# Attention with a mixture of experts on one core: one-hots and low parts move from GpSimd to VectorE, the heads' sums to GpSimd, half of the early weight bounds to ScalarE

## The chip, the cores and the metric

The kernel runs on one NeuronCore of one Trainium2 chip. The core has a matrix engine (TensorE; the profile calls it PE, and its weight loads PEld), VectorE (DVE), ScalarE (ACT), GpSimd (POOL) and SyncE (SP), which issues most DMAs. The metric is the device time of one execution in microseconds (us), as the median of several runs.

## The reference

A windowed attention is followed by a mixture of experts in which each token goes to two of eight experts.

```python
# attention: q, k, v are (8 batches, 8 heads, 576 positions, 64)
scores = scale * q @ k.T                       # per head
mask = (rel >= 0) & (rel < 128)                # rel = query position - key position
scores = where(mask, scores - slope_h * |rel|, -1e9)
attn = softmax(scores);  out = attn @ v
x = out as 4608 tokens of 512                  # heads side by side
# experts
logits = x @ w_gate
noisy = logits + log1p(exp(x @ w_noise)) * noise
top2 = the two largest of 8;  weights = softmax of the two
for e in range(8):                             # w1[e]: 512 x 1024, w2[e]: 1024 x 512
    h = relu(x[tokens of e] @ w1[e])
    out[tokens of e] += weight * (h @ w2[e])
```

## The kernel before, in words

**The order of the work.** The instructions of all engines are laid out by a planner inside the kernel's own code (class `Order`). Every piece of work is a generator, a "strand", that yields operations, each with an engine, a cost in us that the author wrote beside it, and a rank. The planner keeps a clock of its own, and whenever an engine is free by that clock it emits the waiting operation with the lowest rank. The order in which it emits becomes the fixed order of each engine's queue on the chip. An engine works its queue in order, so an operation whose input is late holds up all that stands behind it. The costs and the constants at the top of the file (`GATE`, `ROUTE`, `WEIGHTS`, `STAGE`, `LATE` and so on, which shift ranks) thus set the order, but not how long anything takes. The helper `either` offers an operation to ScalarE and VectorE; the first that is free takes it, and an entry of `LATE` shifts VectorE's rank for it. `move` is a DMA on SP.

**Attention.** There are 32 pairs (a batch and two heads) of three groups of query blocks, 96 units (`unit`). Each unit makes its scores on TensorE (L472, L479), takes tops with the mask and bias on VectorE (L495 to L505), exponentials with their sums on ScalarE (L512), transposes on TensorE (L519), an evacuation on either engine (L261 or L265, into `pT`), a split of the diagonal blocks on GpSimd (`split`, L539 and L540), and the weighted sum of values on TensorE (L560). When all four head pairs of a group are there, `rows` adds a small number to the sums of exponentials on GpSimd (L632) and takes reciprocals on VectorE (L635). Then `row_major` writes the tokens to HBM (L660 to L668), and `gate` makes the logits of each head on TensorE (L683), evacuates and transposes them (L694), multiplies by the reciprocals on VectorE (L699, into `lt`), and adds the eight heads up in one VectorE reduction (L704, into `lg`).

**Routing.** For each of the eight batches, `route` takes the noise and the logits, finds the two best experts and each token's place in the expert's list. The places are written as one-hots, in two parts: which line of the list (80 values, `hot[0]`, L783 and L788) and which place in the line (64 values, `hot[1]`, L793), the latter multiplied by the token's number. For batches 0 to 6 GpSimd makes them in ten operations each, one for each of five token blocks and two choices; for the last batch VectorE makes the lines in one operation and the places in ten. Ten matmuls (`list_`, L798) multiply the two one-hots into lists, which VectorE takes out (`whole_numbers`, L803 to L806) and an indirect DMA adds to the lists in HBM (L877). The planner counts 2.2 us for the lines on GpSimd and 0.4 us for each of five pairs of places.

**Experts.** Weights and tokens are split into a high and a low 16-bit part, and each product is three matmuls (high by high, high by low, low by high). To scale weights into range, the largest absolute value of each expert's `w1` and `w2` is taken first: for experts 0 and 1 by `early_sizes`, 16 pieces of 128x512 each, and for the rest by `size_of_weights`. Each piece is loaded (L1013) and reduced on VectorE (`largest`, L1014); `powers_of_weights` turns the maxima into powers of two (L1029 and on). Then `scaled_weight` loads each chunk f = 0 to 7 of the expert (L1039), makes its high part on ScalarE or VectorE (L261 or L263), and its low part: for expert 0 on GpSimd in two operations (L1045, L1046), for the others on VectorE in one (L1051).

Once six batches are routed, a first wave takes two blocks of 384 tokens of expert 0 and works on them beside the end of attention; the second wave takes all other tokens of all experts. For a block, tokens are gathered by indirect DMA (L1062), scaled (`fit`, L1075 to L1079) and transposed (L1093); L1107 is the first product, L1127, L1129 and L1142 its ReLU in two parts, L1151 or L1156 the second product, and L1228 the indirect DMA that adds the result to the output.

**Ranks that the change and the prediction's steps touch.** A unit's rank is about its place in 160 (five per pair) plus an entry of `STAGE`. Routing of batch b has rank 20b - `ROUTE`. Chunk f of expert 0 has rank `WEIGHTS[0]` + `WEIGHTS[1]` f. The first wave starts at rank `FFN0`, the second at 1000.

Of the kernel before, what the change touches and what calls it, by code (L numbers as in the profile page):

```python
# [21 lines left out]
NQ = 5  # L22
# [18 lines left out]
GATE = (-9.0, -7.0)  # L41
ROUTE = -11.5
SCATTER = (15.0, -1042.6, -45.1)
FFN0, FFN1 = 175.6, 182.4
WEIGHTS = (94.1, 13.2)
TOKENS = 75.6
STAGE = (-14.6, 12.0, 2.3, -11.7, 15.1, 9.4, 15.1, -33.6)
MIDDLE = 41.4
RESULT = -72.8
SIZES = (65.9, 147.7, 901.7)  # L50
EARLY = 2
SOON = 2.3
TIGHT = (1, 5, 7)
LATE = (-8.0, -9.8, 75.9, 24.8, 4.9, -85.3, 60.4, -97.2, 42.9, 0.5, 26.7, -30.3)
LAG = 0.2
SWITCH, NEAR = 0.093, 3.6
# [165 lines left out]
def attention_moe(ctx: ExitStack, tc: tile.TileContext, qk_, v, w_gate, w_noise, noise, w1, w2,  # L222
# [449 lines left out]
    def gate(b, blocks, xu, den, t, done):  # L672
# [19 lines left out]
        def turn():  # L692
# [11 lines left out]
        yield dve(0.36 if nz == 1 else 0.5, rank, lambda: nc.vector.tensor_reduce(  # L704
            lgs[b % 2][0:rows, i:i + nz], lt[0:rows, 0:nz].rearrange("p z h e -> p z e h"), axis=AX.X, op=OP.add))
# [16 lines left out]
    def route(b):  # L722
# [6 lines left out]
        on, G = (dve, nc.vector) if b == B - 1 else (pool, nc.gpsimd)  # L729
# [49 lines left out]
        def which_line():  # L779

            if b == B - 1:
                shape = [128, 2 * NQ, E * SPAN]
                V.tensor_tensor(hot[0], ef.rearrange("p i k -> p (i k)")[:, :, None].to_broadcast(shape),  # L783
                                steps_[:, None, :].to_broadcast(shape), op=OP.is_equal)
                return
            for i in range(NQ):
                for k in range(2):
                    G.tensor_scalar(hot[0][:, 2 * i + k], steps_, ef[:, i, k:k + 1], None, op0=OP.is_equal)  # L788

        def which_place(i):  # L790

            for k in range(2):
                G.tensor_scalar(hot[1][:, 2 * i + k], steps_[:, 0:LINE], d[:, i, k:k + 1], numbers[:, i:i + 1],  # L793
                                op0=OP.is_equal, op1=OP.mult)
# [72 lines left out]
        yield on(0.98 if b == B - 1 else 2.2, rank, which_line)  # L867
        for i in range(NQ):
            yield on(0.4, rank, lambda: which_place(i))
# [16 lines left out]
        if b + 1 == CUT:  # L886
# [11 lines left out]
            for blk in first:  # L898
                blk.ix, blk.at = (v[:, blk.s0 // 128:(blk.s0 + blk.n) // 128] for v in (ix, cl))
                mark(blk.ids)  # L900
                spawn(weights_back(blk, rank))

# [80 lines left out]
    def early_sizes():  # L983

        yield biased[NP - 1]
        for e in range(EARLY):
            done = Event(16)
            for f in range(8):
                for z, (rg, src) in enumerate(((raw1, w1), (raw2, w2))):
                    t = yield (rg, SIZES[e])  # L990
                    v = t.rearrange("p a b -> p (a b)") if z == 0 else t
                    spawn(largest(rg, t, v, 0.6, SIZES[e], wam[:, e % 2, z, f:f + 1],
# [491 lines left out]
```

## Time and profile before

| | us |
|---|---|
| median of 3 runs | 1205.41 (1204.83 to 1205.69) |
| profiled execution, its own time | 1203.02 |
| its span, first to last instruction | 1201.1 |
| TensorE busy | 1111.9, 93% |
| VectorE busy | 696.6, 58% |
| ScalarE busy | 493.9, 41% |
| GpSimd busy | 432.4, 36% |
| mean granted TensorE clock | 0.968 of full |

The profile is one execution, so sums over its rows are held against its own time of 1203.02 us, not against the median. In rows of groups the columns are line, engine, operation, output and inputs by the program's names with shapes, count; then busy us and mean ns of one; then the idle time of the engine just before these instructions and who ended it. Rows of waits read: who waited for whom, us in total, times, longest. Rows of the timeline begin with start and length in us. In the views by instruction a row gives least, median and greatest duration in ns and the first and last start. A matmul's duration overlaps the next one's.

### The profile page before, as it was taken

The numbers are of one execution on the slowest core, as the hardware profiler recorded it, in microseconds if no ns is written. First come the engines' busy times: TensorE is split into PE (matmuls) and PEld (weight loads), VectorE is DVE, ScalarE is ACT, GpSimd is POOL, SyncE is SP. The second block draws the span as 40 slices with busy tenths as digits, with TensorE's granted clock in tenths as the row PEclk, the third lists the DMA queues.
The fourth block names the chain that finished last, engine by engine and source line by source line (L and its number), as shares of the span: only waits on it lengthen the run. The fifth ranks groups of instructions, "written<-read, shape, count | busy, mean of one in ns | idle before, by whom it ended". The sixth has DMA issues, their size and how long they took to land.

```text
span 1201.1 us, 20775 instructions
## 1 busy us (share of the span) xinstructions
PE 1111.9 (93%) x7192; PEld 649.4 (54%) x7192; DVE 696.6 (58%) x2491; ACT 493.9 (41%) x1327; POOL 432.4 (36%) x676
## 2 busy tenths in 40 slices
PE   7988789876799999999999999999999999999995
PEld 5765556554445444574566456545645654575552
DVE  7989688876666357257535734672584457252310
ACT  7775566644243235133532423342343324232311
POOL 3458978876350230222322032221313220222211
PEclk9999898889799999999999999999999999999998
DMA  8887786412256356335824553472456342332221
GB/s 310 284 285 275 241 306 229 131 45 77 59 122 193 62 141 193 63 75 142 233 40 125 159 126 63 132 218 40 103 173 171 63 132 89 63 62 45 35 27 23
DMA packets 115418, 160.76 MB, mean 134 GB/s; under 512 B 24688, under 2 KB 67952, under 8 KB 115312
## 3 DMA queue, kind: packets, MB, share of 16 engines
q1 hardware_dynamic: 97392, 119.09, 30.4%
q0 software_dynamic: 17920, 40.33, 17.8%
q8 instruction: 57, 0.93, 0.3%
q14 instruction: 49, 0.40, 0.1%
HBM read 117.99 MB, written 41.40 MB: 133 GB/s over the span
## 4 chain that ended last, share of the span: by engine, by line
PE 60%; DMA 5%; DVE 5%; issue 1%; ACT 0%; POOL 0%; another core or an unknown queue 0%; POOLq 0%; DVEq 0%; ACTq 0%
PE bank L1107 28%; PE bank L1151 21%; PE bank L1156 8%; DMA mraw<-in_w_dram 4%; PE bank L1093 2%; DVE wam L1014 2%; DMA raw<-in_w_dram 1%; DVE xl L1100 0%; DMA xg<-xs_dram,ix 0%; PE bank L1209 0%; DVE hl L1142 0%; DMA xg<-xs_dram,cl 0%; DVE yo L263 0%; DVE fit L1079 0%; POOL out_dram L1228 0%
## 5 line engine op out<-in xcount | busy, mean ns | idle before, releaser
L1228 POOL DMA_INDIRECT out_dram<-yo,ix x74 | 116.7, 1577 | 591.5 <-ACT yo L261 438.1
L1142 DVE SCALAR_TENSOR_TENSOR hl<-bank,hh 128x384 f16<-128x384 f32 (+3 forms) x192 | 110.8, 578 | 296.1 <-ACT hh L1127 295.7
L1127 ACT ACTIVATE hh<-bank 128x512 f16<-128x512 f32 (+3 forms) x171 | 87.5, 512 | 364.5 <-PE bank L1107 363.2
L1151 PEld LDWEIGHTS <-hh 128*128 128x128 f16 (+1 forms) x928 | 89.4, 98 | 96.6 <-issue 5.8
L1107 PE MATMUL bank<-xh,w1hb 128*128 128x320 f16 (+2 forms) x384 | 129.9, 338 | 0.0
L1107 PE MATMUL bank<-xl,w1hb 128*128 128x320 f16 (+2 forms) x384 | 129.9, 338 | 0.0
L1107 PE MATMUL bank<-xh,w1lb 128*128 128x320 f16 (+2 forms) x384 | 129.8, 338 | 0.0
L1107 PE MATMUL bank<-xl,w1ha 128*128 128x384 f16 (+3 forms) x384 | 129.7, 338 | 0.0
L1107 PE MATMUL bank<-xh,w1ha 128*128 128x384 f16 (+3 forms) x384 | 129.7, 338 | 0.0
L1107 PE MATMUL bank<-xh,w1la 128*128 128x384 f16 (+3 forms) x384 | 129.7, 338 | 0.0
L512 ACT ACTIVATE p<-p,nm 128x128 f32<-128x128 f32 x288 | 111.6, 391 | 13.2 <-DVE nm L505 13.2
L1107 PEld LDWEIGHTS <-w1ha 128*128 128x128 f16 x768 | 75.3, 99 | 57.4 <-issue 2.8
L1107 PEld LDWEIGHTS <-w1hb 128*128 128x128 f16 x768 | 75.3, 99 | 55.9 <-issue 3.4
L1151 PE MATMUL bank<-w2ha,hl 128*128 128x512 f16 (+1 forms) x234 | 89.3, 382 | 1.2 <-DVE hl L1142 1.2
L1151 PE MATMUL bank<-w2ha,hh 128*128 128x512 f16 (+1 forms) x234 | 89.4, 382 | 0.0
L1151 PE MATMUL bank<-w2la,hh 128*128 128x512 f16 (+1 forms) x234 | 89.3, 382 | 0.0
L1151 PE MATMUL bank<-w2hb,hh 128*128 128x512 f16 x230 | 87.3, 379 | 0.5 <-ACT hh L1127 0.5
L1151 PE MATMUL bank<-w2hb,hl 128*128 128x512 f16 x230 | 87.2, 379 | 0.5 <-DVE hl L1142 0.5
L1151 PE MATMUL bank<-w2lb,hh 128*128 128x512 f16 x230 | 87.2, 379 | 0.0
L560 PE MATMUL bank<-pT,vraw 128*64 128x128 f32 (+2 forms) x896 | 76.4, 306 | 9.6 <-POOL pT L540 9.6
L1062 POOL DMA_INDIRECT xg<-xs_dram,ix x74 | 72.4, 979 | 34.1 <-issue 15.2
L479 PE MATMUL bank<-qk 64*128 64x256 f32 (+1 forms) x512 | 72.4, 404 | 12.8 <-DMA qk<-in_qk_dram 6.5
(220 smaller groups left out, 2173.6 us busy)
## 6 DMA issues: line engine op xcount, KB each, us to landing
raw<-in_w_dram SPq DMA_DIRECT2D x160, 256.0 KB, 4.0
mraw<-in_w_dram SPq DMA_DIRECT2D x48, 512.0 KB, 6.2
qk<-in_qk_dram SPq DMA_DIRECT2D x32, 608.0 KB, 4.9
vraw<-in_v_dram SPq DMA_DIRECT2D x16, 640.0 KB, 6.1
out_dram<-xg SPq DMA_DIRECT2D x10, 1024.0 KB, 7.7
xs_dram<-x SPq DMA_DIRECT2D x32, 256.0 KB, 4.0
xg<-xs_dram,ix POOLq DMA_INDIRECT x74, 4.4
out_dram<-yo,ix POOLq DMA_INDIRECT x74, 5.1
```

The lines of the kernel that those rows point to most:

```text
L479: nc.tensor.matmul(s[h][:, o:o + c], qk[half, i * 128:i * 128 + 128], qk[half, QW + k0:QW + k0 + c], start=True, stop=True)
L512: nc.scalar.activation(pv, pv, AF.Exp, bias=nm[:, z, h:h + 1], scale=-1.0, accum_out=den[:, z, 2 * g + h:2 * g + h + 1])
L560: nc.tensor.matmul(o[half, o0:o0 + c], t[:, kb, hh:hh + D], w, start=m == 0, stop=m == len(lst) - 1)
L1014: yield dve(us, rank, lambda: nc.vector.tensor_reduce(o, v, axis=AX.X, op=OP.max, apply_absolute_value=True))
L1062: yield pool(1.04, rank, lambda: nc.gpsimd.indirect_dma_start(out=xg[0:r], out_offset=None, in_=xs[0:blk.rows], in_offset=bass.IndirectOff ...
L1093: nc.tensor.transpose(a[:, c * 128:c * 128 + r], xg[0:r, c * 128:c * 128 + 128], ident[0:r, 0:r])
L1107: nc.tensor.matmul(t[:, 0:blk.n], wp[:, c], x[:, c, 0:blk.n], start=c == 0 and z == 0, stop=c == 3 and z == 2)
L1127: nc.scalar.activation(o, i, AF.Relu)
L1142: yield dve(0.07 + c * 0.00104, rank - MIDDLE, lambda: nc.vector.scalar_tensor_tensor(hl[:, 0:c], t[:, 0:c], 0.0, hh[:, 0:c], op0=OP.max, ...
L1151: nc.tensor.matmul(blk.y[j][0:r], h[:, cs], wp, start=f == 0 and m == 0, stop=f == 7 and m == 2)
L1156: nc.tensor.matmul(blk.y[c][:, 0:blk.n], wp[:, c * 128:c * 128 + 128], h[:, 0:blk.n], start=f == 0 and m == 0, stop=f == 7 and m == 2)
L1228: ins = nc.gpsimd.indirect_dma_start(out=out, out_offset=bass.IndirectOffsetOnAxis(ap=blk.ix[0:r, j:j + 1], axis=0), in_=t[0:r], in_offset ...
```

## The change

It has five parts, and new values for the constants.

- One-hots: for all batches, VectorE makes the lines in one operation over 10 x 80 values and the places in one over 10 x 64. The numbers are multiplied in by one GpSimd operation (by VectorE in the last batch), in a strand of its own (`number_them`) so that VectorE's lines don't wait for it; the list matmuls wait for both.
- Heads: the eight heads' logits are added up on GpSimd in three additions (8 to 4 to 2 to 1) in place of VectorE's reduction.
- Early bounds: for `w2` of experts 0 and 1, ScalarE takes the sum of absolute values of each row piece in place of VectorE's maximum. A sum is an upper bound of the maximum; the powers of two for these are shifted by 12 to make up for it.
- Low parts of expert 0: made on VectorE in one operation, as for the other experts.
- Costs given to the planner for these, and the constants.

```diff
-GATE = (-9.0, -7.0)
-ROUTE = -11.5
-SCATTER = (15.0, -1042.6, -45.1)
-FFN0, FFN1 = 175.6, 182.4
-WEIGHTS = (94.1, 13.2)
-TOKENS = 75.6
-STAGE = (-14.6, 12.0, 2.3, -11.7, 15.1, 9.4, 15.1, -33.6)
-MIDDLE = 41.4
+GATE = (-9.0, -1.1)
+ROUTE = 3.6
+SCATTER = (15.0, -1042.6, -37.6)
+FFN0, FFN1 = 175.6, 176.6
+WEIGHTS = (97.0, 72.2)
+TOKENS = 68.4
+STAGE = (-4.9, 8.1, 2.3, -7.2, 3.2, 9.4, 8.5, -33.6)
+MIDDLE = 30.8
...
-SIZES = (65.9, 147.7, 901.7)
+SIZES = (77.9, 147.7, 901.7)
-SOON = 2.3
+SOON = 52.3
-LATE = (-8.0, -9.8, 75.9, 24.8, 4.9, -85.3, 60.4, -97.2, 42.9, 0.5, 26.7, -30.3)
+LATE = (-8.0, -35.3, 75.9, 49.7, 15.7, -92.0, 67.3, -97.2, 22.6, 0.5, 26.7, -30.3)
-SWITCH, NEAR = 0.093, 3.6
+SWITCH, NEAR = 0.093, 4.1
...
-        yield dve(0.36 if nz == 1 else 0.5, rank, lambda: nc.vector.tensor_reduce(
-            lgs[b % 2][0:rows, i:i + nz], lt[0:rows, 0:nz].rearrange("p z h e -> p z e h"), axis=AX.X, op=OP.add))
+        def sum_of_heads():
+            for c in (4, 2):
+                v = lt[0:rows, 0:nz, 0:c]
+                nc.gpsimd.tensor_tensor(v, v, lt[0:rows, 0:nz, c:2 * c], op=OP.add)
+            nc.gpsimd.tensor_tensor(lgs[b % 2][0:rows, i:i + nz], lt[0:rows, 0:nz, 0], lt[0:rows, 0:nz, 1], op=OP.add)
+        yield pool(0.7 if nz == 1 else 0.9, rank, sum_of_heads)
...
-        on, G = (dve, nc.vector) if b == B - 1 else (pool, nc.gpsimd)
+        on, G, us = (dve, V, 0.75) if b == B - 1 else (pool, nc.gpsimd, 1.5)
...
         def which_line():
-            if b == B - 1:
-                shape = [128, 2 * NQ, E * SPAN]
-                V.tensor_tensor(hot[0], ...)
-                return
-            for i in range(NQ):
-                for k in range(2):
-                    G.tensor_scalar(hot[0][:, 2 * i + k], steps_, ef[:, i, k:k + 1], None, op0=OP.is_equal)
-        def which_place(i):
-            for k in range(2):
-                G.tensor_scalar(hot[1][:, 2 * i + k], steps_[:, 0:LINE], d[:, i, k:k + 1], numbers[:, i:i + 1],
-                                op0=OP.is_equal, op1=OP.mult)
+            shape = [128, 2 * NQ, E * SPAN]
+            V.tensor_tensor(hot[0], ef.rearrange("p i k -> p (i k)")[:, :, None].to_broadcast(shape),
+                            steps_[:, None, :].to_broadcast(shape), op=OP.is_equal)
+        def which_place():
+            shape = [128, 2 * NQ, LINE]
+            V.tensor_tensor(hot[1], d.rearrange("p i k -> p (i k)")[:, :, None].to_broadcast(shape),
+                            steps_[:, None, 0:LINE].to_broadcast(shape), op=OP.is_equal)
+        def numbered():
+            t = hot[1].rearrange("p (i k) c -> p i (k c)", k=2)
+            G.tensor_tensor(t, t, numbers[:, :, None].to_broadcast([128, NQ, 2 * LINE]), op=OP.mult)
...
-        yield on(0.98 if b == B - 1 else 2.2, rank, which_line)
-        for i in range(NQ):
-            yield on(0.4, rank, lambda: which_place(i))
+        yield dve(0.75, rank, which_place)
+        spawn(number_them(on, us, rank, numbered, ready := Event()))
+        yield dve(0.98, rank, which_line)
+        yield ready
...
+    def number_them(on, us, rank, numbered, ready):
+        yield on(us, rank, numbered)
+        mark(ready)
...
-                    spawn(largest(rg, t, v, 0.6, SIZES[e], wam[:, e % 2, z, f:f + 1],
-                                  dram(src, e * DM * F + f * 65536, [[512, 128], [1, 512]]), done))
+                    spawn(largest(rg, t, v, (0.6, 0.7)[z], SIZES[e], wam[:, e % 2, z, f:f + 1],
+                                  dram(src, e * DM * F + f * 65536, [[512, 128], [1, 512]]), done, z))
...
-    def largest(rg, t, v, us, rank, o, src, done):
+    def largest(rg, t, v, us, rank, o, src, done, sum_=False):
         yield from move(5.2e5, rank, lambda: nc.sync.dma_start(v, src))
-        yield dve(us, rank, lambda: nc.vector.tensor_reduce(o, v, axis=AX.X, op=OP.max, apply_absolute_value=True))
+        if sum_:
+            yield act(us, rank, lambda: nc.scalar.activation(v, v, AF.Abs, accum_out=o))
+        else:
+            yield dve(us, rank, lambda: nc.vector.tensor_reduce(o, v, axis=AX.X, op=OP.max, apply_absolute_value=True))
...
         def powers():
-            V.tensor_scalar(wsc[:, e], wex[:, e], -1.0, float(256 << 23), op0=OP.mult, op1=OP.add)
-            V.tensor_scalar(wex[:, e], wex[:, e], float(-2 << 23), None, op0=OP.add)
+            for z, more_ in ((slice(0, 1), 0), (slice(1, 2), 12)) if e < EARLY else ((slice(0, 2), 0),):
+                V.tensor_scalar(wsc[:, e, z], wex[:, e, z], -1.0, float(256 + more_ << 23), op0=OP.mult, op1=OP.add)
+                V.tensor_scalar(wex[:, e, z], wex[:, e, z], float(-2 - more_ << 23), None, op0=OP.add)
...
-        def rest_of_weight():
-            nc.gpsimd.tensor_scalar(t, t, sc, None, op0=OP.mult)
-            nc.gpsimd.tensor_tensor(lo, t, hi, op=OP.subtract)
-        if e == 0:
-            yield pool(1.9, rank, rest_of_weight)
-        else:
-            yield dve(0.66, rank, lambda: nc.vector.scalar_tensor_tensor(lo, t, sc, hi, op0=OP.mult, op1=OP.subtract))
+        yield dve(0.6, rank, lambda: nc.vector.scalar_tensor_tensor(lo, t, sc, hi, op0=OP.mult, op1=OP.subtract))
```

More of the change, by code (lines that the diff above doesn't have):

```diff
@@ L779, in which_line @@
         def which_line():
-            if b == B - 1:
-                shape = [128, 2 * NQ, E * SPAN]
-                V.tensor_tensor(hot[0], ef.rearrange("p i k -> p (i k)")[:, :, None].to_broadcast(shape),
-                                steps_[:, None, :].to_broadcast(shape), op=OP.is_equal)
-                return
-            for i in range(NQ):
-                for k in range(2):
-                    G.tensor_scalar(hot[0][:, 2 * i + k], steps_, ef[:, i, k:k + 1], None, op0=OP.is_equal)
-        def which_place(i):
-            for k in range(2):
-                G.tensor_scalar(hot[1][:, 2 * i + k], steps_[:, 0:LINE], d[:, i, k:k + 1], numbers[:, i:i + 1],
-                                op0=OP.is_equal, op1=OP.mult)
+            shape = [128, 2 * NQ, E * SPAN]
[8 more added lines that the diff above has]
+            G.tensor_tensor(t, t, numbers[:, :, None].to_broadcast([128, NQ, 2 * LINE]), op=OP.mult)
         def list_(a):
```

## The prediction

> **What bounds the kernel now.** I read the page first: the engines' shares, and where in the span TensorE is short of full.
>
> ```profile
> span 1201.1 us, 20775 instructions
> ...
> PE 1111.9 (93%) x7192; PEld 649.4 (54%) x7192; DVE 696.6 (58%) x2491; ACT 493.9 (41%) x1327; POOL 432.4 (36%) x676
> ...
> PE   7988789876799999999999999999999999999995
> POOL 3458978876350230222322032221313220222211
> PEclk9999898889799999999999999999999999999998
> ```
>
> TensorE is busy for 93% of the span, so the kernel can only get shorter where TensorE is idle or where its clock is below full. Each digit is 30 us. Both losses lie mostly in the first twelve digits, the attention part with routing; that is where GpSimd has its 7, 8 and 9. The averages (GpSimd 36%) hide this. So I cut that part into stretches and read them one by one (columns: length; busy time and count of TensorE, its weight loads, VectorE, ScalarE, GpSimd; granted clock; DMA share; GB/s).
>
> ```profile
> 60.00:310.00 250.00, 204.25 (x1905) 137.03 (x1904) 201.99 (x1049) 147.72 (x615) 187.03 (x338) 0.90 0.58 192
> 120.00:140.00 20.00, 13.48 (x87) 9.17 (x86) 9.34 (x44) 9.77 (x42) 19.37 (x33) 0.74 0.69 232
> 140.00:170.00 30.00, 29.07 (x300) 20.38 (x299) 28.83 (x158) 22.16 (x96) 21.99 (x38) 1.00 0.92 305
> 180.00:190.00 10.00, 9.03 (x67) 6.04 (x68) 7.22 (x36) 5.69 (x26) 9.34 (x22) 0.68 0.80 275
> 190.00:200.00 10.00, 9.12 (x93) 6.35 (x90) 9.82 (x56) 7.55 (x28) 9.45 (x13) 1.00 0.47 147
> 220.00:230.00 10.00, 8.58 (x59) 5.50 (x60) 7.16 (x37) 4.48 (x17) 9.49 (x21) 0.66 0.28 96
> 230.00:250.00 20.00, 19.98 (x204) 13.67 (x205) 19.06 (x117) 14.33 (x64) 13.15 (x25) 1.00 0.36 101
> 260.00:270.00 10.00, 7.64 (x54) 4.88 (x54) 6.41 (x36) 2.36 (x9) 7.58 (x16) 0.66 0.14 29
> 290.00:310.00 20.00, 10.20 (x75) 6.31 (x73) 14.49 (x66) 4.98 (x11) 3.01 (x3) 0.64 0.33 100
> ```
>
> There are two kinds of stretch. In 140 to 170, 190 to 200 and 230 to 250 the work flows: TensorE is idle for 1.83 of 60 us, its clock is full, and VectorE is busy for 57.71 of 60 us, 96%. In 120 to 140 GpSimd is busy for 19.37 of 20 us, VectorE for less than half, TensorE for two thirds, and the clock is at 0.74. The stretches at 180, 220 and 260 have the same low clock, and GpSimd leads VectorE in each. So two limits alternate: VectorE where it flows, GpSimd where it does not. The waits name what GpSimd is late with:
>
> ```profile
> PE bank L798 <- POOL hot L793: 12.5, 15, 4.9
> PE bank L560 <- POOL pT L540: 9.6, 8, 3.2
> PE bank L479 <- DVE nm L505: 6.2, 7, 2.0
> DVE den L635 <- POOL den L632: 7.4, 5, 2.6
> ```
>
> TensorE stands 12.5 us at L798, the matmuls that turn one-hots into lists, because GpSimd has not made the one-hots; and 9.6 us at L560 for the splits of L540, which queue on GpSimd behind the same work. VectorE itself stands 7.4 us for a small GpSimd operation (L632). One such place in the timeline, with the reason:
>
> ```profile
> 117.96 0.68 PE L798 MATMUL bank<-hot,hot 128*80 128x64 f16 x8
> 123.58 0.21 PE L798 MATMUL bank<-hot,hot 128*80 128x64 f16 x1 [4.94 <-POOL hot L793]
> ...
> L793 POOL TENSOR_SCALAR hot<-steps,d,numbers 128x64 f16<-128x64 f16 x70 | 40.0, 592 | 0.5
> L788 POOL TENSOR_SCALAR hot<-steps,ef 128x80 f16<-128x80 f16 x70 | 33.0, 489 | 24.7 <-DVE ef L764 24.6
> ```
>
> The planner that lays the order counts 2.2 us for the ten operations of L788 and five times 0.4 us for the ten of L793, 4.2 us a batch. The rows say 10 x 0.489 + 10 x 0.592 = 10.8 us. The order puts the list matmuls where the one-hots should be done, and they come up to 6.6 us later; TensorE takes its queue in order, so it waits with work behind it.
>
> **The change part by part.** First what leaves GpSimd and what comes to it, then VectorE.
>
> ```profile
> L1045 POOL TENSOR_SCALAR raw<-raw,wsc 128x512 f32<-128x512 f32 x16 | 25.5, 1592 | 4.4 <-DVE lo L761 2.8 <-DVE w1ha L263 1.1 <-DVE both L823 0.4
> L1046 POOL TENSOR_TENSOR w1la<-raw,w1ha x8: 1157/1162/1207, 78.2 to 214.1; 128x512 f16<-128x512 f32 x8
> L1046 POOL TENSOR_TENSOR w2la<-raw,w2ha x8: 1156/1158/1191, 81.0 to 231.5; 128x512 f16<-128x512 f32 x8
> L632 POOL TENSOR_SCALAR den<-den 128x16 f32<-128x16 f32 (+1 forms) x24 | 6.2, 260 | 2.0
> L704 DVE TENSOR_REDUCE lg<-lt 128x32 f32<-128x256 f32 (+1 forms) x24 | 11.9, 501 | 0.0
> L1014 DVE TENSOR_REDUCE wam<-raw 128x1 f32<-128x512 f32 x32 | 21.1, 673 | 0.0
> L1014 DVE TENSOR_REDUCE wam<-mraw 128x1 f32<-128x1024 f32 x48 | 58.3, 1214 | 19.3 <-DMA mraw<-in_w_dram 19.3
> L1051 DVE SCALAR_TENSOR_TENSOR w1lb<-raw,wsc,w1hb 128x512 f16<-128x512 f32 x32 | 23.9, 746 | 3.9 <-ACT w1hb L261 3.7
> L261 ACT ACTIVATE xg<-xg,fit 128x512 f32<-128x512 f32 (+1 forms) x77 | 54.6, 718 | 32.8 <-DVE fit L1075 32.4
> ```
>
> GpSimd loses 33.0 + 40.0 us of one-hots (batches 0 to 6) and the low parts of expert 0, 25.5 + 16 x 1.16 = 44.1 us: 117.1 us in all. It gains 24 sums of heads, three dependent additions each over 128, 64 and 32 elements a partition (half of that for the short group), and seven multiplications by the numbers over 640 elements. The trace shows no such addition; between L632 (16 elements, 0.26 us) and L1046 (512 elements, 1.16 us) the line rises by 1.81 ns an element, so a sum costs 0.46 + 0.35 + 0.29 = 1.1 us (0.78 if all were as L632, 3.48 if as L1046), 24 of them at most 26.4 us; a multiplication 1.39 us (1.16 to 1.45), seven 9.7 us. Net: 81 us less of the 187.03 in 60 to 310, which takes GpSimd from 75% to 42%.
>
> VectorE loses the 24 reductions of L704, 11.9 us, and half of the 32 size reductions, 16 x 0.673 = 10.8 us. It gains the low parts of expert 0, 16 x 0.746 = 11.9 us, and for seven batches one operation over 800 elements and one over 640. The last batch already makes its lines in that form:
>
> ```profile
> 321.78 1.15 DVE L783 TENSOR_TENSOR hot<-ef,steps 128x800 f16<-128x800 f32 x1
> ...
> 174.64 4.61 POOL L788 TENSOR_SCALAR hot<-steps,ef 128x80 f16<-128x80 f16 x10
> ...
> 318.52 5.21 POOL L788 TENSOR_SCALAR hot<-steps,ef 128x80 f16<-128x80 f16 x10 [24.23 <-DVE ef L764]
> ```
>
> So 7 x 1.15 + 7 x 0.92 = 14.5 us, and VectorE's net is +3.7 us. The last batch's places, two operations for ten of the same elements, and the two small operations added where the powers are taken (two experts) I count at nothing. ScalarE gains 16 absolute sums of 512 elements, 0.718 us each by the row of the same shape, 11.5 us. ScalarE is busy for 147.72 of 250 us and these sums have no reader until all sixteen are done, so nothing; uncovered, 11.5 us. No DMA is added or taken; the order in which SP issues them moves with the constants. Two waits are new: a low part on VectorE waits for its high part with the score tops behind it, which free TensorE's score banks (the 6.2 us wait of L479 is of that kind); and routing's first ScalarE step now waits for GpSimd's sum.
>
> One price is special to the mix. From 512 to 1024 elements L1014 rises by 0.541 us, 1.06 ns an element, so 800 elements should take 0.98 us; L783 took 1.15, 0.17 more. It ran at 321.78, inside the ten GpSimd operations that began at 318.52 and took 5.21 us where the ten at 174.64 took 4.61. I price the 30 new VectorE operations with two SBUF operands at 0.17 each, 5.1 us (0 to 18.0, if each cost the 0.60 that GpSimd lost). The Trainium skill (SBUF — State Buffer, section "SBUF: two separate sides") states a rule that speaks against this change: VectorE and GpSimd share a pair of ports that is locked for a whole instruction, also by a VectorE operation with two SBUF inputs against a GpSimd operation that reads SBUF, and the loser blocks fully. The trace agrees in direction: both sides were late at once, by 0.17 and 0.60 us; no other such pair of these shapes is in it.
>
> Now the path. Gone are the direct waits, 12.5 + 9.6 = 22.1 us. Gone with them is the slow clock of the stretches at 120, 180, 220 and 260: busy time by missing clock is 0.26 x 13.48 + 0.32 x 9.03 + 0.34 x 8.58 + 0.34 x 7.64 = 11.9 us. Together -34.0. Against it: VectorE is what is late next, since it is at 96% where the work flows, so its +3.7 and the 5.1 beside GpSimd count in full, +8.8. Some waits for GpSimd stay. A split now queues behind at most about 1.4 us instead of 4.61, or behind a sum of heads that itself waits at the head of GpSimd's queue for VectorE's product; I keep 9.6 x 1.4 / 4.61 = 2.9. The planner's new costs for the one-hots (0.75 + 0.98 + 1.5) stand against 0.92 + 1.15 + 1.39, 0.23 us short, 1.6 us over seven lists. Sum: -34.0 + 8.8 + 4.5 = -20.7 us. VectorE would then be busy for about 211 of 229 us, 92%, between today's 81% and the 96% of the flowing stretches: possible, not slack.
>
> The retuned constants (routing earlier, expert 0's later weights much later, second tokens earlier, other ranks) I count at nothing; their ends are the second and third rivals. From 345 us on nothing but order changes, and TensorE's digits are 9s there: nothing. The profiled execution took 1203.02 us, 1.9 beyond its span and 2.4 under the median; -20.7 gives 1182.3 there and 1205.41 - 20.7 = 1184.7 for the median.
>
> **The rivals.** (1) VectorE binds sooner. It reaches only 88%, halfway between 81 and 96: 211 / 0.88 = 240 us instead of 250, so -10: 1195. For it: the new order has more on VectorE where it is full already. Against: in 60 us of this trace it held 96%.
>
> (2) The earlier routing of batch 5 also closes the gap at 290 to 310, where TensorE is idle for 9.8 us and loses 0.36 x 10.20 = 3.7 to the clock while the first tokens are fetched. Then -20.7 - 13.5: 1171. For it: batch 5's one-hots alone come several us sooner and its rank is 15 lower. Against: attention ends sooner too, and the chain through list, fetch and transposes is as long as before.
>
> (3) Slower: expert 0's weights come too late. Chunks had ranks from 94 to 187 and the last low part was begun at 231.5; now chunk 2 has rank 241 and chunk 7 has 602, behind all attention units (at most about 175). A chunk needs its load, high part and low part:
>
> ```profile
> raw<-in_w_dram SPq DMA_DIRECT2D x160, 256.0 KB, 4.0
> ...
> 374.35 2.70 PE bank L1151 x12
> 377.04 3.41 PE bank L1107 x21
> ```
>
> That is 4.0 + 0.72 + 0.75 = 5.5 us in series. Two blocks of 384 use a chunk for 24 matmuls of L1107 (0.162 us each) and 18 of L1151 (0.225), 7.9 us, so one chunk ahead hides it. It decides once VectorE and ScalarE, full with the end of attention and routing, no longer deliver the 2 x (0.72 + 0.75) us of conversions per 7.9 us: six chunks exposed are 33 us, 1205.4 - 20.7 + 33 = 1218.
>
> (4) The shared ports, the rule of the page named above, taken at the upper price: 18.0 instead of 5.1 us, of which GpSimd's slack takes some; all of it on the path gives 1198.
>
> (5) The change doesn't do what it says: the stalls only change names, since TensorE's queue is in order and some other step is mis-timed at the same places: 1205.
>
> **How the numbers follow.** My forecast, the stalls at the one-hots go: 0.50. Rival 1: 0.14. Rival 2: 0.14. Rival 3: 0.11. Rival 4: 0.04. Rival 5: 0.07, of which 0.05 is no change and 0.02 slower. A measurement of this kernel can tell about 0.2%, 2.4 us, from no change. Faster: 0.50 + 0.14 + 0.14 + 0.04 = 0.82; same 0.05; slower 0.11 + 0.02 = 0.13. The range goes down to 1165 (all of the 34.0 and half of the 13.5) and up to 1206; it leaves out rival 3 and a little below.
>
> **What would show it.** Right: no wait of TensorE at the list matmuls above 1 us, GpSimd at 40 to 50% in 60 to 310, VectorE above 88% there, granted clock at 0.95 or more, one-hot operations of VectorE near 1.15 and 0.92 us, and the same busy time and gaps as now in the second wave. Wrong: the list wait is back under another releaser; VectorE's waits for GpSimd grow with the heads' sums; the first L1107 matmuls wait for `raw` loads or low parts; or TensorE's idle time in 60 to 310 (45.75 us) falls by less than 10.

## The result, and the profile after

The changed kernel takes 1164.15 us (median of 4 runs, 1163.22 to 1164.69) against 1205.31 (1204.83 to 1205.69, 4 runs) beside it: a ratio of 0.9658, 95% interval 0.9641 to 0.9675. That is 41 us less, where 20.7 were forecast, and 0.85 us below the low end of the range. All ratios are of fast executions; one of the four of after_heads_on_vector, below, was a slow one of 6279 us and is not in its ratio. The profiled execution took 1164.45 us, 1.75 beyond its span. The same rows of the page as in the prediction:

```profile
span 1162.7 us, 20693 instructions
...
PE 1098.4 (94%) x7192; PEld 643.7 (55%) x7192; DVE 688.6 (59%) x2470; ACT 505.1 (43%) x1366; POOL 356.4 (31%) x583
...
PE   7979998899889999999999999999999999999995
POOL 3535655573412113320232223133203321232211
PEclk9989998999989999999999999999999999999998
```

The span is 38.4 us shorter. TensorE's idle time fell from 89.2 to 64.3 us (span less busy time), 24.9 of it, and its busy time, for the same 7192 matmuls, by 13.5. Of GpSimd's 7s, 8s and 9s in the first ten digits a single 7 is left, and TensorE's 7, 6, 7 in the ninth to eleventh digit (240 to 330 us) are 9, 9, 8. The two stretches that the prediction cut out, in the columns given there:

```profile
60.00:310.00 250.00, 224.42 (x2103) 148.51 (x2100) 221.29 (x1142) 164.89 (x654) 126.28 (x270) 0.96 0.62 203
290.00:310.00 20.00, 18.01 (x98) 9.22 (x97) 13.88 (x52) 9.11 (x16) 6.07 (x7) 0.98 0.52 136
```

GpSimd went from 187.03 to 126.28 us (51%, where 40 to 50 were forecast), VectorE from 201.99 to 221.29 (89%), TensorE's idle time from 45.75 to 25.58, the clock from 0.90 to 0.96. Busy time by missing clock is 224.42 x 0.04 = 9.0 us, where it was 204.25 x 0.10 = 20.4. In 290 to 310 TensorE now works, since its expert matmuls have begun. The waits of TensorE:

```profile
PE bank L560 <- POOL pT L540: 4.5, 8, 1.0
...
PE bank L519 <- ACT gt L261: 2.9, 1, 2.9
PE bank L752 <- DVE both L828: 2.4, 1, 2.4
...
PE bank L479 <- DVE nm L505: 0.7, 2, 0.4
...
PE bank L803 <- DVE hot L788: 0.6, 2, 0.3
...
PE bank L803 <- DVE lt L699: 0.5, 1, 0.5
```

The list matmuls (L803 now) wait 1.1 us instead of 12.5, the values' matmuls (L560) 4.5 for the splits instead of 9.6, the scores 0.7 instead of 6.2. The waits at L519 (a transpose) and L752 (a matmul of routing) are new. Where the time went is best read from three points: the last matmul of attention (L560), the first of the experts, and the end. First the kernel before, by the view of two lines' instructions (the last two numbers ahead of the shapes are the first and the last start in us):

```profile
L560 PE MATMUL bank<-pT,vraw x896: 219/273/690, 14.5 to 288.3; 128*64 128x128 f32 x78, 128*64 128x256 f32 x51, 128*64 128x64 f32 x51
...
L1107 PE MATMUL bank<-xh,w1ha x384: 299/326/524, 308.0 to 1177.5; 128*128 128x384 f16 x80, 128*128 128x512 f16 x48, 128*128 128x320 f16 x48, 128*128 128x448 f16 x16
```

Then the changed kernel:

```profile
L560 PE MATMUL bank<-pT,vraw x896: 219/273/690, 14.4 to 268.4; 128*64 128x128 f32 x78, 128*64 128x256 f32 x51, 128*64 128x64 f32 x51
...
L1114 PE MATMUL bank<-xh,w1ha x384: 299/326/528, 271.0 to 1139.3; 128*128 128x384 f16 x80, 128*128 128x512 f16 x48, 128*128 128x320 f16 x48, 128*128 128x448 f16 x16
```

Attention ends 19.9 us earlier (288.3 to 268.4). From there to the first expert matmul it was 19.7 us and is 2.6, 17.1 less. From there to the end it was 893.1 and is 891.7, 1.4 less. These three make the 38.4.

### The profile page after: what moved, and what is told of

Read it like the earlier page. It is cut to its first block, busy times and chain, and to the rows that moved or that the text cites. A ratio compares the mean times of both kernels' runs of the same rounds, so it can differ in the third digit from the quotient of the medians.

```text
span 1162.7 us, 20693 instructions
## 1 busy us (share of the span) xinstructions
PE 1098.4 (94%) x7192; PEld 643.7 (55%) x7192; DVE 688.6 (59%) x2470; ACT 505.1 (43%) x1366; POOL 356.4 (31%) x583
## 4 chain that ended last, share of the span: by engine, by line
PE 64%; DMA 4%; DVE 3%; issue 1%; POOL 1%; ACT 0%; POOLq 0%; another core or an unknown queue 0%; DVEq 0%
PE bank L1114 30%; PE bank L1158 22%; PE bank L1163 8%; DMA mraw<-in_w_dram 3%; PE bank L1100 3%; DVE wam L1028 2%; DMA xg<-xs_dram,ix 1%; PE bank L1216 1%; POOL out_dram L1235 0%; DMA xg<-xs_dram,cl 0%; DVE hl L1149 0%; DVE xl L1107 0%; DVE yo L263 0%; DVE fit L1086 0%; POOL xg L1069 0%
## 5 line engine op out<-in xcount | busy, mean ns | idle before, releaser
L1134 ACT ACTIVATE hh<-bank 128x384 f16<-128x384 f32 (+3 forms) x185 | 94.3, 510 | 377.4 <-PE bank L1114 354.5
L1158 PE MATMUL bank<-w2ha,hl 128*128 128x512 f16 (+1 forms) x234 | 89.2, 381 | 1.7 <-DVE hl L1149 1.7
L1158 PE MATMUL bank<-w2la,hh 128*128 128x512 f16 (+1 forms) x234 | 89.2, 381 | 0.0
L261 ACT ACTIVATE xh<-bank 128x512 f16<-128x512 f32 (+1 forms) x79 | 45.3, 573 | 84.2 <-PE bank L1100 84.1
L560 PE MATMUL bank<-pT,vraw 128*64 128x128 f32 (+2 forms) x896 | 74.7, 304 | 6.0 <-POOL pT L540 4.5
```

The costliest lines, as they stand in the source:

```text
L261: nc.scalar.activation(o, i, AF.Copy, **kw)
L560: nc.tensor.matmul(o[half, o0:o0 + c], t[:, kb, hh:hh + D], w, start=m == 0, stop=m == len(lst) - 1)
L1134: nc.scalar.activation(o, i, AF.Relu)
L1158: nc.tensor.matmul(blk.y[j][0:r], h[:, cs], wp, start=f == 0 and m == 0, stop=f == 7 and m == 2)
```

## The experiments

The theories. **Work**: GpSimd is relieved of the one-hots and low parts, so TensorE's stalls in attention go; the constants only follow. **Constants**: the new ranks bring the lists forward and close the gap ahead of the experts. **Costs**: the one-hots cost time less by their load than because the planner was told 4.2 us for 10.8. **Fit**: the constants were tuned to one exact order, and another order, whatever its work, loses a few us.

The table has all kernels. Columns: ratio to the kernel before on the same chip with its 95% interval; then from the profile, in us, the span, the start of GpSimd's indirect DMA for the sixth list (after which the first wave may begin), the last start of L560 (attention's end), the first expert matmul. The times are of the one profiled execution, the ratio is of all; in after_nudge_split that execution was 6.7 us faster than its median, in before_nudge_soft 4.2.

| kernel | ratio | span | sixth list | attention's end | first expert matmul |
|---|---|---|---|---|---|
| before | 1 | 1201.1 | 280.6 | 288.3 | 308.0 |
| after | 0.9658 (0.9641 to 0.9675) | 1162.7 | 244.7 | 268.4 | 271.0 |
| work_alone | 0.9793 (0.9767 to 0.9819) | 1178.2 | 260.8 | 267.9 | 288.0 |
| consts_alone | 1.0029 (1.0010 to 1.0049) | 1206.1 | 289.9 | 297.6 | 317.2 |
| before_nudge_soft | 1.0078 (1.0052 to 1.0103) | 1209.1 | 295.9 | 294.3 | 317.1 |
| before_nudge_split | 1.0089 (1.0065 to 1.0112) | 1217.5 | 291.2 | 291.3 | 317.5 |
| after_nudge_soft | 0.9735 (0.9710 to 0.9761) | 1174.4 | 258.6 | 277.2 | 284.2 |
| after_nudge_split | 0.9741 (0.9705 to 0.9777) | 1165.3 | 251.8 | 263.4 | 280.2 |
| costs_alone | 0.9918 (0.9893 to 0.9944) | 1193.7 | 276.0 | 281.5 | 306.5 |
| onehots_alone | 0.9860 (0.9832 to 0.9888) | 1189.5 | 258.7 | 279.5 | 284.8 |
| after_onehots_on_gpsimd | 1.0003 (0.9981 to 1.0024) | 1205.5 | 290.4 | 298.3 | 314.7 |
| after_onehots_on_gpsimd_true | 0.9818 (0.9773 to 0.9862) | 1184.7 | 273.2 | 281.9 | 299.3 |
| after_old_route | 0.9725 (0.9690 to 0.9759) | 1169.8 | 251.4 | 270.3 | 274.6 |
| work_new_route | 0.9736 (0.9716 to 0.9756) | 1170.1 | 249.6 | 269.9 | 275.2 |
| after_low_on_gpsimd | 0.9784 (0.9764 to 0.9804) | 1183.0 | 266.5 | 284.5 | 292.3 |
| after_heads_on_vector | 0.9725 (0.9676 to 0.9775) | 1173.3 | 251.6 | 278.1 | 278.5 |
| after_sizes_on_vector | 0.9773 (0.9735 to 0.9811) | 1176.8 | 254.7 | 275.9 | 278.6 |
| work_heads_on_vector | 0.9839 (0.9807 to 0.9871) | 1180.8 | 267.0 | 272.0 | 289.2 |
| work_sizes_on_vector | 0.9774 (0.9740 to 0.9808) | 1179.9 | 260.1 | 264.3 | 285.3 |
| after_true_costs | 0.9686 (0.9647 to 0.9725) | 1167.8 | 246.4 | 270.3 | 272.8 |

Span less first expert matmul is 885 to 900 us in all but one (onehots_alone, 905), while the first expert matmul moves from 271 to 318. And it comes 21 to 31 us behind the sixth list in every kernel. So the span follows the sixth list: less the start of that, it is 911 to 926 us in all but onehots_alone (931). Attention's end alone does not tell it: after_nudge_split ends attention first of all, at 263.4, and starts its experts at 280.2. So the questions for each are when attention ends, and how far ahead of that end the sixth list goes out: 7.7 us before, 23.7 after.

### Work and constants apart

work_alone is the changed kernel, its costs included, with all the old constants. consts_alone is the old work with the new constants.

```diff
 work_alone, against after
-GATE = (-9.0, -1.1)
-ROUTE = 3.6
+GATE = (-9.0, -7.0)
+ROUTE = -11.5
...
 consts_alone, against before
-ROUTE = -11.5
+ROUTE = 3.6
...
```

> The changed kernel's work and planner costs under the old constants. Theory 1 (the moved work ends the waits behind GpSimd, about 21 us; the retuned constants close the gap before the first wave, about 17 us): 1182 to 1190, list wait of TensorE under 2 us, and 10 us or more between the last value matmul of attention and the first expert matmul. Rival (the work alone brings it all, the constants next to nothing): 1164 to 1170. Rival (the constants are what counts, since each order fits its own constants): 1200 or more.

> The old work and planner costs under the new constants. Theory 1: the one-hots on GpSimd still make TensorE wait 10 us or more for the lists, the earlier routing shortens the gap before the first wave by some us: 1190 to 1203. Rival (constants count): 1164 to 1185. Rival (constants fit only the new work): 1206 or more, up to 1225.

Measured: 0.9793 for the work alone, 25 us; 1.0029 for the constants alone, 3.5 us slower. The first is 2 us under the range of theory 1, with its gap of over 10 us; its list matmuls wait 2.7 us where under 2 were expected. The second misses theory 1 (1190 to 1203) and fits the rival by which the new constants fit only the new work. In work_alone:

```profile
L560 PE MATMUL bank<-pT,vraw x896: 219/273/689, 14.3 to 267.9; 128*64 128x128 f32 x78, 128*64 128x256 f32 x51, 128*64 128x64 f32 x51
...
L1114 PE MATMUL bank<-xh,w1ha x384: 299/326/527, 288.0 to 1154.4; 128*128 128x384 f16 x80, 128*128 128x512 f16 x48, 128*128 128x320 f16 x48, 128*128 128x448 f16 x16
```

With the work alone attention ends at 267.9, as early as in the changed kernel, and the gap to the experts stays: 20.1 us, beside 19.7 before and 2.6 after. So the work makes the earlier end of attention and leaves the gap; with the constants added, the gap closes. In the timeline of work_alone, and then of the changed kernel, the sixth list goes out at:

```profile
260.80 1.50 POOL L883 DMA_INDIRECT slots_dram<-listed,line_of  x1 [1.63 <-DVE listed L811]
```

```profile
244.69 1.50 POOL L883 DMA_INDIRECT slots_dram<-listed,line_of  x1 [0.16 <-DVE bank L500]
```

The 16.1 us between these make up most of the 17.0 between the first expert matmuls. With the old work the new constants do nothing of the kind: the list is again 7.7 us ahead of an end that itself comes 9.3 us later, and the list matmuls wait 15.0 us for the one-hots of batches that are now ranked 15.1 lower (20b - `ROUTE`).

### Two small nudges

Two costs that the planner counts, changed by 2 to 4%, give another order of exactly the same work. Each was made on the kernel before and on the changed one.

```diff
 nudge_soft
-... SOFT, SPLIT = ... (1.56, 1.56, 0.4), (0.85, 1.35, 0.6)
+... SOFT, SPLIT = ... (1.6, 1.6, 0.4), (0.85, 1.35, 0.6)
 nudge_split
+... SOFT, SPLIT = ... (1.56, 1.56, 0.4), (0.87, 1.38, 0.62)
```

> The changed kernel with no work changed: the planner's cost of the exponentials is 1.60 instead of 1.56 us, which lays the whole attention in another order. If the constants are fitted to one exact order, a meaningless nudge loses 8 to 15 us as each undone part did: 1172 to 1180. If undone parts lost by their own work: 1161 to 1168.

> As the other nudge, with the planner's cost of the splits 0.87, 1.38 and 0.62 instead of 0.85, 1.35 and 0.60. Fitted order: 1172 to 1180. Own work: 1161 to 1168.

> The old kernel with the planner's cost of the exponentials 1.60 instead of 1.56 us, no work changed. If the old constants were fitted to their order as the new ones are: 1212 to 1220, and the moved work is worth more than the 25 us that it brought under them. If not: 1200 to 1208, and the constants' share of the gain is a gain of its own.

> As the other, with the planner's cost of the splits 0.87, 1.38 and 0.62. Fitted: 1212 to 1220. Not: 1200 to 1208.

All four lost: 1.0078 and 1.0089 before, 0.9735 and 0.9741 after, which is 0.0083 and 0.0080 (10.0 and 9.6 us) above the kernel that was nudged. They came within the ranges expected of constants that fit one order, and I put about 10 us down to that fit. This is not shown apart from another reading: the planner's 1.56 is four exponentials at the 0.39 us of the trace, so the nudged 1.60 is also a less true cost. And not every new order lost as much: consts_alone lost 3.5 us and after_true_costs, below, 3.4, each with something else changed too. The change compares fit with fit, work_alone and consts_alone compare an unfitted kernel with a fitted one. Like with like, if swapped constants lose as much as a nudge (which no run shows), against the nudged kernel before (1.0083), the work gives 0.9793 - 1.0083 = -0.0290, 35 us; the constants' own share is 0.9738 - 0.9793 = -0.0055 with the new work and 1.0029 - 1.0083 = -0.0054 with the old, 6.6 and 6.5 us. 35 + 6.6 is the 41. With two nudges a side and intervals of 0.2 to 0.4% to either side, each of these is good to some 4 us at best, and they are estimates: what the runs show directly is 25 us with the work and 16.3 more with the constants on top.

### The one-hots: load or wrong durations

costs_alone tells the planner what the profile measured and moves no work. onehots_alone is the kernel before with the new one-hots (and their costs) only. The third takes the one-hots of the changed kernel back to GpSimd with the old costs, the fourth does so with the measured ones.

```diff
 costs_alone, against before (after_onehots_on_gpsimd_true has the first two)
-        yield on(0.98 if b == B - 1 else 2.2, rank, which_line)
+        yield on(0.98 if b == B - 1 else 4.9, rank, which_line)
-            yield on(0.4, rank, lambda: which_place(i))
+            yield on(0.4 if b == B - 1 else 1.18, rank, lambda: which_place(i))
-            yield pool(1.9, rank, rest_of_weight)
+            yield pool(2.75, rank, rest_of_weight)
...
 onehots_alone, against before (after_onehots_on_gpsimd undoes these in after)
-            for i in range(NQ):
-                for k in range(2):
-                    G.tensor_scalar(hot[0][:, 2 * i + k], steps_, ef[:, i, k:k + 1], None, op0=OP.is_equal)
+            V.tensor_tensor(hot[0], ef..., steps_..., op=OP.is_equal)
```

> The old kernel in which only three numbers that the planner is told are changed to what the trace measured: lines 4.9 us, each pair of places 1.18, low part of expert 0 2.75; the instructions are the same, in another order. If the loss came from the order being laid with wrong durations: TensorE's list wait falls from 12.5 to under 4 us and the time to 1185 to 1195. If it came from GpSimd having too much to do: list wait falls but the time stays within 5 us of 1205, with the waits under other names.

> The old kernel and constants with the one-hots alone changed (VectorE in two operations, numbers on GpSimd, new planner costs). Theory 1: list wait under 2 us; the one-hots are 73 of the 117 us taken from GpSimd, so most of the 21 us: 1188 to 1195. Rival (VectorE, full where the work flows, pays the 14.5 us back): 1198 to 1206.

> The changed kernel with the one-hots back on GpSimd as before, with the planner's old costs for them. If they are the main part of the gain: TensorE's list wait is back at 8 to 15 us, 1185 to 1200. If the low parts are as important: 1172 to 1180.

> The changed kernel with the one-hots back on GpSimd, but the planner told what they take (4.9 us for the lines, 1.18 for each pair of places). If the loss of these one-hots is that the order was laid for shorter operations: half or more of the 41 us comes back, 1176 to 1187, list wait under 3 us. If it is GpSimd's load as such: 1192 to 1207, with waits for splits.

Three numbers in the planner are worth 9.9 us (0.9918), 19.9 against the nudged kernel before; one of the three is the low parts' cost. At 1195.84 the run lies just past the range for wrong durations (1185 to 1195) and outside the one for load. Its 9.9 us are no more than a nudge moves, so it needs the run from the other side, below. GpSimd does all its old work in costs_alone:

```profile
60.00:310.00 250.00, 203.14 (x1945) 137.17 (x1942) 218.99 (x1120) 148.19 (x615) 199.85 (x361) 0.90 0.60 198
```

It is busy for 199.85 of 250 us, more than before. Yet the wait at the lists is gone from TensorE's waits, and what is left is the rest of the same queue:

```profile
PE bank L560 <- POOL pT L540: 12.1, 8, 5.9
PE bank L479 <- DVE nm L505: 9.7, 12, 2.5
```

From the other side: with the one-hots back on GpSimd the whole gain is lost (1.0003), and TensorE waits

```profile
PE bank L560 <- POOL pT L540: 20.6, 13, 3.6
...
PE bank L804 <- POOL hot L799: 6.9, 13, 1.3
```

in the kernel with the old costs (1207.17, beyond the 1185 to 1200 that was expected, and more for the splits than for the lists), but with the measured ones

```profile
PE bank L560 <- POOL pT L540: 13.0, 11, 5.6
...
PE bank L804 <- POOL hot L799: 0.9, 2, 0.5
```

and hardly at the lists. That gives back 1.0003 - 0.9818, 22 us, with only the costs different, and twice what a nudge moves. Of the 19.3 us that remain about 10 are a misfit by the estimate from the nudges, and about 10 the load itself, the splits queueing on GpSimd. By that estimate, of the one-hots' own loss of some 32 us two thirds were the order laid with 4.2 us for 10.8 (22 here, 20 from the kernel before, with the low parts' cost in it), and one third was GpSimd's load. onehots_alone (0.9860, 17 us; 27 against the nudged kernel; 1188 to 1195 expected, 1189.1 measured) is the largest part of the change by itself.

### The routing's ranks

```diff
 after_old_route, against after (work_new_route is the reverse, against work_alone)
-GATE = (-9.0, -1.1)
-ROUTE = 3.6
-SCATTER = (15.0, -1042.6, -37.6)
+GATE = (-9.0, -7.0)
+ROUTE = -11.5
+SCATTER = (15.0, -1042.6, -45.1)
```

> The changed kernel with three constants of the old one, those that rank routing and the logits before it. If earlier routing is what closes the gap before the first wave: the sixth list goes out near 260 instead of 245, the first expert matmul moves from 271 to 283 or later, 1174 to 1182. If the gap closes by other constants (tokens, first-wave ranks, stages): 1164 to 1169.

> The new work under the old constants, but with the three new routing ranks. If these three alone carry the constants' share: 1164 to 1170 with the gap at 2 to 5 us. If the constants only act together: 1176 or more.

On top of the work alone the three routing constants bring 0.9736 against 0.9793, 6.9 us, with an interval that ends below the other's begin: the sixth list goes out at 249.6 instead of 260.8, and the gap falls from 20.1 to 5.3. Taken out of the changed kernel they cost 8.1 us, no more than a nudge, and the gap is still only 4.3, with the sixth list at 251.4 where near 260 was expected. onehots_alone has a gap of 5.3 with all the old constants. Both runs fell between the ranges of their rivals. So the earlier routing closes the gap, but it isn't the only order that does.

### The smaller parts

Each is undone in the changed kernel; heads and bounds also in work_alone, whose constants fit neither version.

```diff
 after_low_on_gpsimd
+        if e == 0:
+            yield pool(1.9, rank, rest_of_weight)
 heads_on_vector
-        yield pool(0.7 if nz == 1 else 0.9, rank, sum_of_heads)
+        yield dve(0.36 if nz == 1 else 0.5, rank, lambda: nc.vector.tensor_reduce(...))
 sizes_on_vector
-                    spawn(largest(rg, t, v, (0.6, 0.7)[z], ..., done, z))
+                    spawn(largest(rg, t, v, 0.6, ..., done))
```

> The changed kernel with the low parts of expert 0 back on GpSimd. They take 44 us of GpSimd and give 12 back to VectorE. If GpSimd, at half load without them, has room now: 1160 to 1168, or faster since VectorE is full. If they stand in front of splits as the one-hots did: 1170 to 1180.

> The changed kernel with the heads added up by one VectorE reduction again. By the count of VectorE's time (11.9 us back on it, full in this stretch): 1168 to 1176. If the additions on GpSimd cost as much as they bring (GpSimd waited 25 us at the head of its queue for their input, splits behind it): 1158 to 1165.

> The changed kernel with the bounds of w2 of experts 0 and 1 taken by VectorE's maximum again, 10.8 us back on VectorE and 13 off ScalarE. By VectorE's time: 1168 to 1175. If they lie in idle time of either engine: 1162 to 1167.

> The new work under the old constants (1180 by the earlier run), with the heads added up on VectorE again. If the move of the heads is worth its 11.9 us on a full VectorE: 1186 to 1194. If its loss under the new constants was a matter of the order: 1176 to 1184.

> The new work under the old constants, with the bounds of w2 on VectorE again. If that move is worth its 10.8 us: 1186 to 1194. If its loss under the new constants was a matter of the order: 1176 to 1184.

Undone in the changed kernel they cost 15.2, 8.1 and 13.9 us; the low parts and the bounds lost 2 and 5 us more than the highest that was expected. With the 41.6 of the one-hots the parts sum to 79, twice what they gain together. Less a misfit of about 10 each (the estimate from the nudges), there remain some 5, 0 and 4. Under constants that fit neither version the heads are worth 5.5 us (0.9839 against 0.9793, intervals that overlap at their ends) and the bounds nothing that can be measured (0.9774, 2.3 us the other way). For these two the small sizes stay open. The low parts' own 5 us is this estimate alone. Their row after the undoing shows why a few us are plausible, the queue ahead of the splits:

```profile
PE bank L560 <- POOL pT L540: 8.4, 9, 3.6
```

### The changed kernel with measured costs

```diff
-        yield dve(0.75, rank, which_place)
+        yield dve(0.8, rank, which_place)
-        yield dve(0.98, rank, which_line)
+        yield dve(1.03, rank, which_line)
-... else (pool, nc.gpsimd, 1.5)
+... else (pool, nc.gpsimd, 1.36)
-        yield pool(0.7 if nz == 1 else 0.9, rank, sum_of_heads)
+        yield pool(0.9 if nz == 1 else 1.2, rank, sum_of_heads)
```

> The changed kernel with the planner's costs for its new operations set to what its trace shows (places 0.80, lines 1.03, numbers 1.36, heads 1.2 and 0.9). If truer durations always lay a better order: 1155 to 1162. If constants that were fitted to the old costs count for as much: 1163 to 1175.

0.9686 (0.9647 to 0.9725), not to be told from the changed kernel's 0.9658. The costs that are left to correct are small, and the corrected order has no constants fitted to it; which of the two keeps it from gaining is open. No version tried beats the changed kernel.

## Why the prediction was wrong

**Right: the cause.** TensorE stood behind GpSimd's one-hots and splits, and that went as said: 12.5 to 1.1 us at the lists, 9.6 to 4.5 at L560 (2.9 forecast), 20.4 to 9.0 us of slow clock from 60 to 310 us where 11.9 were to go. Rival 5 did not come, but waits did change names in part: of the 35.96 us that TensorE is idle from 60 us to the end of attention, those for lists, splits and tops take 25.2 (9.6 of the lists' 12.5 fall there), in the changed kernel 6.0 of 22.77. All others grew by 6, with the new ones at L519 and L752. The forecast had in it, as work_alone shows, what the work does to attention: its end came 20.4 us earlier, where the sum was 20.7. That the sizes meet is partly luck. In the changed kernel, by the two rows of windows below, TensorE's idle time up to attention's end fell by 13.2 us and its busy time, for nearly the same matmuls, by 6.8; the sum had 8.8 (22.1 less 8.8 and 4.5) and 11.9.

**Right: the prices.** The rows of the changed kernel, grouped by line and shape:

```profile
L788 DVE TENSOR_TENSOR hot<-ef,steps 128x800 f16<-128x800 f32 x8 | 9.1, 1135 | 0.0
L794 DVE TENSOR_TENSOR hot<-d,steps 128x640 f16<-128x640 f32 x8 | 6.6, 821 | 0.0
L799 POOL TENSOR_TENSOR hot<-hot,numbers 128x640 f16<-128x640 f16 x7 | 9.5, 1358 | 9.4 <-DVE tp L744 7.0 <-DVE hot L794 2.4
L708 POOL TENSOR_TENSOR lt<-lt 128x128 f32<-128x128 f32 x16 | 8.3, 519 | 31.0 <-DVE lt L699 23.2 <-DVE lines L774 4.2 <-DVE base L832 3.4
L708 POOL TENSOR_TENSOR lt<-lt 128x64 f32<-128x64 f32 x16 | 5.5, 341 | 1.3
L709 POOL TENSOR_TENSOR lg<-lt 128x32 f32<-128x32 f32 x16 | 4.7, 293 | 1.3
L1026 ACT ACTIVATE raw<-raw 128x512 f32<-128x512 f32 x16 | 10.0, 624 | 0.0
```

Lines 1.135 us (1.15 forecast), places 0.821 (0.92), numbers 1.358 (1.39), a sum of heads 0.519 + 0.341 + 0.293 = 1.15 (1.1); the absolute sum 0.624 (0.718). Reading its accumulator is a second instruction of about 0.19, but in the timeline the next sum starts 0.62 us behind the last, so it adds nothing:

```profile
28.08 0.62 ACT L1026 ACTIVATE raw<-raw 128x512 f32<-128x512 f32 x1
28.60 0.19 ACT L1026 ACTIVATION_READ_ACCUMULATOR raw<-raw 128x1 f32 x1
28.70 0.62 ACT L1026 ACTIVATE raw<-raw 128x512 f32<-128x512 f32 x1
```

VectorE's net follows from these. Its busy time from 60 us to the end of attention, first before, then after:

```profile
60.00:288.00 228.00, 192.04 (x1808) 129.37 (x1808) 185.72 (x972) 141.85 (x601) 183.35 (x332) 0.92 0.61 202
```

```profile
60.00:268.00 208.00, 185.23 (x1811) 125.66 (x1809) 188.72 (x994) 150.89 (x624) 115.91 (x252) 0.95 0.68 225
```

It is 185.72 of 228 us, 81%, and then 188.72 of 208, 91%: 3.0 us more (3.7 forecast) at the share of 92% that was called possible. So rival 1 (88%) did not come.

**Wrong: the step "the retuned constants … I count at nothing".** The changed kernel is 16.3 us ahead of work_alone (0.9793 - 0.9658); that much is shown. By the estimate from the nudges 9.6 of these are the fit of the constants to the new order, which a retuned kernel has and which the kernel before had too, and 6.6 are their own, the earlier routing by its size. They show at one place, the gap ahead of the experts: 20.1 us with the work alone, 2.6 with the constants. That is rival 2's mechanism at 17.5 us, where 13.5 were priced. It was set up as another way for the whole to go, at a chance of 0.14, and it is a term that adds to the forecast. Its row against, "attention ends sooner too, and the chain … is as long as before", was true and did not decide: the chain is as long as before (27.4 us from sixth list to first expert matmul, now 26.3), but more of it lies beside attention. The sum had counted TensorE's stalls in attention as the path; what starts the experts is the sixth list.

**Undersized: the work itself.** 20.7 us forecast, 22.9 by the spans of work_alone and 25 by its median, by the estimate above about 35 like with like. The forecast had no term for the fit that the old constants lost when the work changed; by the nudges that hides about 10 of the 35. What else was too small can be named in part: the scores' wait for tops (L479), which wasn't in the sum, fell from 6.2 to 2.5 us in work_alone and to 0.7 in the changed kernel. And VectorE's 8.8 was too high: it added 0.17 for the ports to each of 30 operations, but the price of the lines, 1.15, was itself measured beside GpSimd and had the 0.17 in it, and the places' 0.92 was scaled from it, so 14 x 0.17 = 2.4 stood twice; the low parts' 16 x 0.17 = 2.7 never came, since they took 0.746 us or little more, as before. So VectorE's 3.0 stand against 8.8. Whether they counted in full on the path was not measured by itself.

**The other rivals.** Rival 3, the late weights of expert 0: the first product waits 0.8 us for a high and 0.4 for a low part of the tokens, and for no weights. Rival 4, the ports: the lock is there (below), and the time is not that of its upper price; its cost on the path was not measured. VectorE's waits for GpSimd did not grow:

```profile
DVE den L635 <- POOL den L632: 0.6, 2, 0.4
```

It was 7.4 us. The wait that the prediction named as new is there as well:

```profile
POOL lt L708 <- DVE lt L699: 25.1, 10, 5.7
```

GpSimd stands 25.1 us for VectorE's products with the splits behind it, and TensorE's wait for splits still fell, with GpSimd at 51%.

## What to carry to other kernels

Where a planner or a hand lays the order, hold its durations against the profile's first: three corrected numbers were worth 10 us here, and half of what the one-hots seemed to cost (22 of 41.6 us) was their wrong duration. Price a part by where the long bound stage begins, counting back along the chain that releases it, here from the sixth list; two kernels whose attention ended within 0.5 us (work_alone and the changed one) differ by 16 us in all. And compare such kernels only beside a nudge that changes the order and no work, since a nudge alone lost 0.8% here, and the losses of the parts, undone one by one under fitted constants, sum to twice the whole.

## What the runs showed of the hardware

A small GpSimd operation can be held for the whole of a VectorE instruction with two SBUF operands. In the timeline of the changed kernel, VectorE and GpSimd side by side:

```profile
232.04 0.98 DVE L788 TENSOR_TENSOR hot<-ef,steps 128x800 f16<-128x800 f32 x1
...
238.98 0.78 DVE L794 TENSOR_TENSOR hot<-d,steps 128x640 f16<-128x640 f32 x1
```

```profile
232.08 1.05 POOL L632 TENSOR_SCALAR den<-den 128x16 f32<-128x16 f32 x1
...
238.96 0.90 POOL L632 TENSOR_SCALAR den<-den 64x8 f32<-64x8 f32 x1
```

The same line's durations over the whole kernel, least, median and greatest in ns:

```profile
L632 POOL TENSOR_SCALAR den<-den x24: 229/253/1055, 35.5 to 266.5; 128x16 f32<-128x16 f32 x16, 64x8 f32<-64x8 f32 x8
```

L632 has a median of 253 ns and took 1.05 and 0.90 us here, each ending about 0.1 us behind the VectorE operation beside it. The prediction had inferred the lock from 0.17 us more in one operation; these rows show the loser waiting out the whole instruction. The Trainium skill (SBUF — State Buffer, section "SBUF: two separate sides") states that the loser blocks for the whole instruction, and the rows agree. VectorE can be the one that is late as well: its lines, 1.013 us in the median, took 1.67 when they began inside GpSimd's multiplication by the numbers.

```profile
121.32 1.67 DVE L788 TENSOR_TENSOR hot<-ef,steps 128x800 f16<-128x800 f32 x1
...
120.89 1.26 POOL L799 TENSOR_TENSOR hot<-hot,numbers 128x640 f16<-128x640 f16 x1 [0.78 <-DVE hot L794]
```

What the lock costs on the path no run measured by itself.
